# A state-space convolution mixed with a bilinear GLU: the last sums in another order, and the planner's durations as traced

## The chip, the cores and the metric

The kernel runs on one core of one Trainium2 chip. The metric is device time in microseconds (us) from the first to the last moment of one execution on the chip. Runs are repeated and the median is given. Beside the timed runs there is one profiled execution, whose trace records every instruction of every engine: TensorE (PE; its weight loads are listed apart as PEld), VectorE (DVE), ScalarE (ACT), GpSimd (POOL) and SyncE (SP). SP's queue issues most transfers, POOL's queue those that add to what lies in memory. A name that ends in q (SPq, POOLq) is an engine's sequencer, which issues transfers and waits.

## The reference

Two layers work on a sequence of 2048 tokens with 512 channels, and a gate mixes them:

```python
x = A_u                                              # [1, 2048, 512]
g = sigmoid((x * gate_w).sum(-1, keepdims=True))     # one number per token
# layer A: a state-space convolution (S4D), 128 modes per channel
dt = exp(log_dt);  A = -exp(log_A_real) + 1j * A_imag;  C = (C_real + 1j * C_imag) * dt
P = exp((A * dt)[:, :, None] * arange(2048))
K = 2 * einsum("dn,dnl->dl", C, P).real              # a kernel of 2048 taps per channel
a = irfft(rfft(x, 4096) * rfft(K, 4096))[:2048] + x * D_skip
# layer B: a GLU without nonlinearity, 1792 hidden units, on its own input
b = ((B_x @ w_gate) * (B_x @ w_up)) @ w_down
return g * a + (1 - g) * b
```

## The kernel before

**The GLU.** Three products in float32 quality: each operand is split into a rounded high part and a low remainder (`whi`, `wlo`, `xs`, `hh`, `hl`, `dhi`, `dlo`), and three matmuls of 128x128 by 512 replace one. The 14 tiles of the hidden dimension are worked in four groups (3, 3, 4, 4), and within a group the tokens in four chunks of 512, forwards in even groups and backwards in odd ones, so that the last chunk worked is chunk 0 (rows 0 to 3 of the output's `[128, 16, 512]` view, `LAST = 0`). For each chunk and tile there are the products `pg` and `pu`; ScalarE copies `pg` to `h`, VectorE multiplies by `pu`, and the result is split. The `y` products follow, and `evacuate` (line 563) scales them by 1 - g on ScalarE into `acc`. The first group stores `acc` to the output; later groups add to the output with an accumulating transfer from POOL's queue. Only for the last chunk of the last group does `acc` stay on the chip; its four rows are written by `ends` (line 581).

**The convolution.** Channels go in 16 blocks of 32. For each block VectorE and ScalarE build tables of powers (`phases`, `direct_powers`, `x_table`, `v_table`; tiles `t`, `rt`, `ri`, `su`, `di`, `x`, `v`, `sq`), and `k_block` (line 996) multiplies them into the taps `kt`. Four blocks make a channel block of 128 channels. For each of these (q = 0 to 3; "the third" is q = 2, "the fourth" q = 3) a transform in four steps follows: the input's and the taps' first step lies in memory as `su_d` and `sk_d`; `m_second` (line 1113) does the second step for each of four sets T; `m_product` multiplies in the frequency domain; `m_inverse` (line 1171) does the inverse's first step for two sets at once and stores it to `y_d`; `m_last` (line 1213) does the last step from `y_d`, for two halves g = 0 (rows 0 to 7) and g = 1 (rows 8 to 15).

`m_last` makes two banks of PSUM per half. ScalarE copies the odd bank, VectorE forms sum and difference with the even one, the rows are multiplied by the gate (`mix_act` on ScalarE for q < 3, `mix_dve` on VectorE for q = 3), and POOL adds them to the output with an accumulating transfer. For q = 2 and q = 3 half g = 0 is cut in two pieces: rows 0 to 3, which stay on the chip (`late["fin"]`), and rows 4 to 7, which are accumulated. In the trace, `m_last` for q = 2 is `k<-in,w_t` with results in tile `in`; for q = 3 it is `k<-x,w_t`, two groups of 16 matmuls with results in tile `x`. `m_inverse` is `k<-y,w3s`.

**The end.** `ends` loads rows 0 to 3 of the output, as far as they are summed, into `sums` (which takes the tile slot `kt`, 1 MB, by SP's queue), adds the two kept pieces for each row (q = 2 and q = 3, 128 columns each), then `acc`, and stores the row (256 KB, SP's queue).

**What sets the order.** Nothing is issued as the code is read. Every step is handed to a planner (`class Work`, line 165) with its engine, a duration in us, what it reads and writes, and a rank. `Work.run` (line 263) plays the steps through on paper: it takes the step that can start first, then the lower rank, then the earlier one in the code, keeps books of the tile slots, of PSUM banks (four of tag `k` for the convolution) and of one bus for transfers, and so makes one order for each engine. On the chip each engine follows its order, and the framework's semaphores make every step wait for its operands. So a duration in the code changes nothing in the instructions, only the order. `T_STEP` sets the earliest planned start of each GLU step, and `many=` keeps runs of many small matmuls apart. A tag's slots are handed out in the order in which the tiles were made in the code (line 240).

Of the kernel before, what the change touches and what calls it, by code (L numbers as in the profile page):

```python
# [18 lines left out]
P = 128  # L19
# [300 lines left out]
def gated_mix_kernel(  # L320
# [33 lines left out]
    m_su, m_sk, m_y, m_out, m_xs = (work.memory() for _ in range(5))  # L354
# [226 lines left out]
    def ends():  # L581
# [5 lines left out]
            w=[sums, *((m_out, t0 + r) for r in range(4))], dma=1024, rows=range(t0, t0 + 4),  # L587
        )
        for r, acc in ending:
            t = t0 + r  # L590
            for q, (fin, parts) in late["fin"].items():
                add(
                    "dve", 0.25,
                    lambda r=r, q=q, fin=fin: dve.tensor_tensor(
                        out=sums.t[:, r, P * q : P * q + P], in0=sums.t[:, r, P * q : P * q + P],
                        in1=fin.t[:, 4 * (LAST % 2) + r], op=ALU.add,
                    ),
                    r=parts, w=[(sums, (r, q))], rank=0,
                )
# [46 lines left out]
    def u_part(t):  # L646
# [4 lines left out]
        def score_of(j):  # L651
# [3 lines left out]
                "dve", 0.77,  # L655
# [191 lines left out]
    def phases(b):  # L847
# [3 lines left out]
        tt(0.83, lambda: t.t, lambda: per_power(rates()[:, 1]), lambda: per_channel(turns), ALU.mult, [par, m_powers], [t])  # L851
        add("act", 0.77, lambda: act.activation(rt.t, t.t, AF.Identity, bias=shift[:, 0:1]), r=[t, m_const], w=[rt])

        add(
            "dve", 0.83,
# [6 lines left out]
            "act", 2.13 if b % 2 or not b else 0.83, lambda: act.activation(t.t, t.t, AF.Sin, scale=-TWO_PI), w=[t],  # L862
        )
        add(
            "act", 0.83, lambda: act.activation(rt.t, rt.t, AF.Sin, scale=-TWO_PI, bias=half_pi[:, 0:1]), r=[m_const],
# [6 lines left out]
    def direct_powers(b):  # L872
# [4 lines left out]
        for c in range(2):  # L877
            f = t if c else rt
            tt(0.83, lambda c=c: ri.t[:, c], lambda f=f: f.t, ampl, ALU.mult, [f, e], [(ri, c)])
# [72 lines left out]
    def v_table(b):  # L952
# [8 lines left out]
        add("act", 1.28, copies, r=[ri], w=[(v, 2)])  # L961
# [5 lines left out]
        for to, of, n in (((33, 64, 2), (0, 16, 1), 16), ((34, 64, 4), (33, 49, 2), 8)):  # L967
# [11 lines left out]
            us = 0.04 * n + 0.08  # L979
            add("act", 1.15 if n == 16 else 0.73, sq_act, r=src_parts, w=[(v, ("r", k)), sq])  # L980
# [15 lines left out]
    def k_block(b, x, v):  # L996
# [18 lines left out]
        add("act", 0.4, lambda: act.copy(side(1), pv(0)[:, :, :, ::-1]), r=[pk], w=[(kt, (1, b % 4))])  # L1015
        for h, op in enumerate((ALU.add, ALU.subtract)):
            add(
                "dve", 0.4, lambda h=h, op=op: dve.tensor_tensor(out=side(h), in0=pv(1), in1=side(1), op=op),
# [52 lines left out]
    def evict(q, n, us, to, src, r, w):  # L1071

        if q == KT - 1 and n % 2:
            add("dve", us, lambda: dve.tensor_copy(to(), src()), r=r, w=w)
# [12 lines left out]
    def m_load(q, T):  # L1087
# [11 lines left out]
        for w, (src, m) in enumerate(((su_d, m_su), (sk_d, m_sk))):  # L1099
            for p in range(2):  # L1100
                r0 = 64 * p + 16 * T
                add(
                    "pool", 1.2,
# [310 lines left out]
```

## Time and profile before

| | |
|---|---|
| median of 3 runs | 606.57 us (606.55 to 610.38) |
| profiled execution | 608.69 us, its span from first to last instruction 606.9 us |
| TensorE busy | 586.3 us, 97% of the span |
| VectorE busy | 527.0 us, 87% |
| ScalarE busy | 389.8 us, 64% |
| POOL busy | 113.9 us, 19% |
| mean granted TensorE clock | 0.989 |
| transfers | 129.73 MB, 214 GB/s in the mean |

Each view of the profile has its own columns. In order of time: start, duration, engine, line, operation, tile written<-tiles read, shapes, count, and in brackets the idle time of the engine just before with what ended it. In groups: engine, operation, tiles, shapes, count, then busy us and mean ns of one, then idle time before them. In stretches: start:end and length, then for TensorE, weight loads, VectorE, ScalarE and POOL the busy us and in brackets the instructions, then the granted TensorE clock, the transfers' share and GB/s. The chain of waits is followed back from the last instruction and gives start, length and engine of each piece. For transfers: tiles, queue, count, KB of each, and us from issue to landing. Every instruction is recorded under line 119, that of a helper, so tiles tell them apart.

### The profile page before, as it was taken

The numbers are of one execution on the slowest core, as the hardware profiler recorded it, in microseconds if no ns is written. First come the engines' busy times: TensorE is split into PE (matmuls) and PEld (weight loads), VectorE is DVE, ScalarE is ACT, GpSimd is POOL, SyncE is SP. The second block draws the span as 40 slices with busy tenths as digits, with TensorE's granted clock in tenths as the row PEclk, the third lists the DMA queues.
The fourth block names the chain that finished last, engine by engine and source line by source line (L and its number), as shares of the span: only waits on it lengthen the run. The fifth ranks groups of instructions, "written<-read, shape, count | busy, mean of one in ns | idle before, by whom it ended". The sixth has DMA issues, their size and how long they took to land.

```text
span 606.9 us, 15872 instructions
## 1 busy us (share of the span) xinstructions
PE 586.3 (97%) x6500; PEld 444.8 (73%) x6500; DVE 527.0 (87%) x841; ACT 389.8 (64%) x879; POOL 113.9 (19%) x173
## 2 busy tenths in 40 slices
PE   8889999999999999999999999999899999999993
PEld 5657676787877777786687877866688777777772
DVE  6999999999999999999799999979999950775725
ACT  5279688686679588758958665966877423434621
POOL 0011212300201340201324101003424021402101
PEclk9989999999999999999999999999899999999997
DMA  8899978575647796749989827886989269989876
GB/s 278 313 354 341 360 263 326 161 218 162 136 151 206 211 226 192 161 135 283 237 178 228 185 81 192 198 228 178 204 171 234 63 170 343 207 257 232 214 155 121
DMA packets 69276, 129.73 MB, mean 214 GB/s; under 512 B 6868, under 2 KB 35540, under 8 KB 66772
## 3 DMA queue, kind: packets, MB, share of 16 engines
q1 hardware_dynamic: 47476, 88.21, 45.8%
q0 software_dynamic: 21312, 40.38, 33.1%
q8 instruction: 51, 0.84, 0.6%
q14 instruction: 21, 0.17, 0.1%
q10 hardware_dynamic: 416, 0.13, 0.1%
HBM read 73.65 MB, written 55.05 MB: 212 GB/s over the span
## 4 chain that ended last, share of the span: by engine, by line
PE 67%; DVE 16%; DMA 10%; issue 4%; ACT 2%; POOLq 0%; SPq 0%; ACTq 0%; DVEq 0%; POOL 0%
PE pg L119 19%; PE pu L119 18%; PE y L119 17%; PE k L119 13%; DMA raw<-in_wts 5%; DVE v L119 3%; DVE x L119 2%; DMA y_d<-e 2%; DMA dt_d<-small 2%; DVE wlo L119 1%; DVE y L119 1%; DVE ri L119 1%; DVE t L119 1%; DVE m L119 1%; DMA x<-dt_d 1%
## 5 line engine op out<-in xcount | busy, mean ns | idle before, releaser
L119 PE MATMUL pg<-xs,whi 128*128 128x512 f32 x448 | 140.1, 394 | 0.5 <-ACT whi L119 0.4
L119 PE MATMUL pu<-xs,whi 128*128 128x512 f32 x448 | 138.2, 390 | 0.0
L119 PEld LDWEIGHTS pg<-xs,whi 128*128 128x128 f32 x448 | 85.0, 190 | 19.8 <-ACT whi L119 1.9
L119 PEld LDWEIGHTS pu<-xs,whi 128*128 128x128 f32 x448 | 84.1, 188 | 17.0
L119 PE MATMUL pg<-xs,wlo 128*128 128x512 f32 x224 | 90.2, 403 | 4.3 <-ACT h L119 3.8
L119 PE MATMUL y<-dhi,hl 128*128 128x512 f32 x224 | 91.1, 407 | 2.9 <-ACT acc L119 1.8
L119 PE MATMUL y<-dlo,hh 128*128 128x512 f32 x224 | 88.2, 394 | 1.6 <-DVE dlo L119 1.6
L119 PE MATMUL pu<-xs,wlo 128*128 128x512 f32 x224 | 89.6, 400 | 0.0
L119 PE MATMUL y<-dhi,hh 128*128 128x512 f32 x224 | 87.9, 393 | 0.0
L119 POOL DMA_DIRECT2D out<-acc x44 | 38.7, 918 | 243.3 <-ACT acc L119 204.7
L119 ACT COPY ev<-k 128x512 f32<-128x512 f32 x112 | 59.2, 594 | 17.2 <-PE k L119 17.2
L119 ACT CAST hh<-h 128x512 fp32r<-128x512 f32 x56 | 34.8, 621 | 44.6 <-DVE h L119 44.4
L119 PEld LDWEIGHTS y<-dhi,hl 128*128 128x128 f32 x224 | 42.4, 189 | 24.3 <-issue 7.8
L119 ACT ACTIVATE acc<-y,ngate 128x512 f32<-128x512 f32 x63 | 42.7, 688 | 25.6 <-PE y L119 20.6
L119 PEld LDWEIGHTS pg<-xs,wlo 128*128 128x128 f32 x224 | 42.5, 190 | 21.5 <-ACT h L119 6.8
L119 PEld LDWEIGHTS pu<-xs,wlo 128*128 128x128 f32 x224 | 42.0, 188 | 15.7 <-issue 7.0
L119 ACT COPY h<-pg 128x512 f32<-128x512 f32 x56 | 32.9, 587 | 31.5 <-PE pg L119 26.1
L119 DVE TENSOR_TENSOR h<-pu,h 128x512 f32<-128x512 f32 x56 | 38.6, 689 | 16.6 <-PE pu L119 15.4
L119 PEld LDWEIGHTS y<-dlo,hh 128*128 128x128 f32 x224 | 42.4, 189 | 9.8 <-DVE dlo L119 1.9
L119 PEld LDWEIGHTS y<-dhi,hh 128*128 128x128 f32 x224 | 42.5, 190 | 9.2
L119 DVE TENSOR_TENSOR hl<-h,hh 128x512 fp32r<-128x512 f32 x56 | 38.5, 688 | 3.7 <-ACT hh L119 3.4
L119 POOL DMA_DIRECT2D su_d<-ev x32 | 17.4, 550 | 96.4 <-ACT ev L119 96.4
(124 smaller groups left out, 1004.2 us busy)
## 6 DMA issues: line engine op xcount, KB each, us to landing
xs<-xs_d SPq DMA_DIRECT2D x36, 512.0 KB, 6.0
out<-acc POOLq DMA_DIRECT2D x44, 256.0 KB, 6.4
raw<-in_wts SPq DMA_DIRECT2D x36, 256.0 KB, 3.7
xs_d<-xs SPq DMA_DIRECT2D x16, 512.0 KB, 7.9
su_d<-ev POOLq DMA_DIRECT2D x32, 256.0 KB, 6.1
y_d<-ts SPq DMA_DIRECT2D x14, 512.0 KB, 4.9
in<-su_d POOLq DMA_DIRECT2D x24, 256.0 KB, 7.9
sk_d<-ev SPq DMA_DIRECT2D x6, 1024.0 KB, 5.6
```

Source lines behind the costliest of these rows:

```text
L119: got = getattr(self.engine, name)(*args, **kw)
```

## The change

- A marker `m_turn` is written by each `m_inverse` and read by `m_last` of q = 2, which so comes after the second `m_inverse` of q = 3.
- In `m_last` the piece that is accumulated (rows 4 to 7) comes ahead of the kept one (rows 0 to 3). The kept pieces are no longer multiplied by the gate; `ends` does that together with the sum, in one `scalar_tensor_tensor` per row and channel block.
- For q = 3 the loads from `y_d` for half g = 1 stand ahead of those for g = 0.
- The load of `sums` comes after the first `y_d` store of q = 3.
- Some fifteen durations that the planner is given are changed.

```diff
--- before.py
+++ after.py
@@ -351,7 +351,7 @@
     sk_d = dram.tile([KT, P, 32, P], F32, name="sk_d")
     y_d = dram.tile([KT, P, 32, P], F32, name="y_d")
     xs_d = dram.tile([4, KT, P, 2, D], F32, name="xs_d")
-    m_su, m_sk, m_y, m_out, m_xs = (work.memory() for _ in range(5))
+    m_su, m_sk, m_y, m_out, m_xs, m_turn = (work.memory() for _ in range(6))
 
     pools = {n: open_pool(n, b, PSUM) for n, b in (("ps_y", 2), ("ps_g", 1), ("ps_k", 4))}
     const = open_pool("const")
@@ -584,18 +584,18 @@
         sums = new("tab", "kt", [P, 4, D])
         add(
             "sp", 0.42, lambda: sp.dma_start(sums.t, ov[:, t0 : t0 + 4, :]),
-            w=[sums, *((m_out, t0 + r) for r in range(4))], dma=1024, rows=range(t0, t0 + 4),
+            r=[(m_y, (KT - 1, 0))], w=[sums, *((m_out, t0 + r) for r in range(4))], dma=1024, rows=range(t0, t0 + 4),
         )
         for r, acc in ending:
             t = t0 + r
             for q, (fin, parts) in late["fin"].items():
                 add(
                     "dve", 0.25,
-                    lambda r=r, q=q, fin=fin: dve.tensor_tensor(
-                        out=sums.t[:, r, P * q : P * q + P], in0=sums.t[:, r, P * q : P * q + P],
-                        in1=fin.t[:, 4 * (LAST % 2) + r], op=ALU.add,
+                    lambda r=r, q=q, t=t, fin=fin: dve.scalar_tensor_tensor(
+                        sums.t[:, r, P * q : P * q + P], fin.t[:, 4 * (LAST % 2) + r], gate[:, t : t + 1],
+                        sums.t[:, r, P * q : P * q + P], op0=ALU.mult, op1=ALU.add,
                     ),
-                    r=parts, w=[(sums, (r, q))], rank=0,
+                    r=[*parts, (m_gate, LAST)], w=[(sums, (r, q))], rank=0,
                 )
             add(
                 "dve", 0.69,
@@ -652,7 +652,7 @@
             r = 4 * t + j
             pr = new("mid", "y", [P, D], bufs=2)
             add(
-                "dve", 0.77,
+                "dve", 0.73,
                 lambda: dve.scalar_tensor_tensor(
                     pr.t, ut.t[:, j, :], 1.0, gw.t, op0=ALU.mult, op1=ALU.mult, accum_out=gate[:, r : r + 1]
                 ),
@@ -848,21 +848,21 @@
 
         t, rt = (new("tab", n, FULL) for n in ("t", "rt"))
         par, rates = pars[b][0]
-        tt(0.83, lambda: t.t, lambda: per_power(rates()[:, 1]), lambda: per_channel(turns), ALU.mult, [par, m_powers], [t])
-        add("act", 0.77, lambda: act.activation(rt.t, t.t, AF.Identity, bias=shift[:, 0:1]), r=[t, m_const], w=[rt])
+        tt(0.85, lambda: t.t, lambda: per_power(rates()[:, 1]), lambda: per_channel(turns), ALU.mult, [par, m_powers], [t])
+        add("act", 0.86, lambda: act.activation(rt.t, t.t, AF.Identity, bias=shift[:, 0:1]), r=[t, m_const], w=[rt])
 
         add(
-            "dve", 0.83,
+            "dve", 0.85,
             lambda: dve.scalar_tensor_tensor(t.t, rt.t, ROUND, t.t, op0=ALU.subtract, op1=ALU.subtract),
             r=[rt], w=[t],
         )
 
         add("act", 0.77, lambda: act.activation(rt.t, t.t, AF.Abs), r=[t], w=[rt])
         add(
-            "act", 2.13 if b % 2 or not b else 0.83, lambda: act.activation(t.t, t.t, AF.Sin, scale=-TWO_PI), w=[t],
+            "act", 2.07 if b % 2 or not b else 0.77, lambda: act.activation(t.t, t.t, AF.Sin, scale=-TWO_PI), w=[t],
         )
         add(
-            "act", 0.83, lambda: act.activation(rt.t, rt.t, AF.Sin, scale=-TWO_PI, bias=half_pi[:, 0:1]), r=[m_const],
+            "act", 0.85, lambda: act.activation(rt.t, rt.t, AF.Sin, scale=-TWO_PI, bias=half_pi[:, 0:1]), r=[m_const],
             w=[rt],
         )
         polar[b] = t, rt
@@ -876,7 +876,7 @@
         ri = ris[b] = new("tab", "ri", [P, 2, TB, NP])
         for c in range(2):
             f = t if c else rt
-            tt(0.83, lambda c=c: ri.t[:, c], lambda f=f: f.t, ampl, ALU.mult, [f, e], [(ri, c)])
+            tt(0.85, lambda c=c: ri.t[:, c], lambda f=f: f.t, ampl, ALU.mult, [f, e], [(ri, c)])
 
         su, di = sus[b] = new("tab", "su", [P, TB, 18]), new("tab", "di", [P, TB, 11])
         re, im = (lambda a, c=c: ri.t[:, c, :, a:18] for c in range(2))
@@ -958,7 +958,7 @@
                 act.copy(v.t[:, c, :, 0:4], ri.t[:, c, :, W_B])
                 act.copy(v.t[:, c, :, 36::4], ri.t[:, c, :, W_A])
 
-        add("act", 1.28, copies, r=[ri], w=[(v, 2)])
+        add("act", 1.46, copies, r=[ri], w=[(v, 2)])
         outer(
             v, lambda: ri.t[:, :, :, W_A], lambda: su.t[:, :, W_A], lambda: ri.t[:, :, :, W_B],
             lambda: su.t[:, :, W_B], lambda: di.t[:, :, 0:4], [ri, su, di],
@@ -976,8 +976,8 @@
 
             k = 0 if n == 16 else 1
             src_parts = [(v, ("r", 0)), (v, ("i", 0))] if k else [(v, 0), (v, 1), (v, 2)]
-            us = 0.04 * n + 0.08
-            add("act", 1.15 if n == 16 else 0.73, sq_act, r=src_parts, w=[(v, ("r", k)), sq])
+            us = 0.69 if n == 16 else 0.63
+            add("act", 1.17 if n == 16 else 0.89, sq_act, r=src_parts, w=[(v, ("r", k)), sq])
             add(
                 "dve", us,
                 lambda dst=dst, src=src: dve.scalar_tensor_tensor(
@@ -1012,10 +1012,10 @@
         add("pe", 2.15, kgen, r=[x, v], w=[pk], rank=0, hold=[kt], many=work.APART)
         pv = lambda a: pk.t.rearrange("p (g a b k) -> p g a b k", a=2, b=2, k=16)[:, :, a]
         side = lambda h: kt.t[:, h, :, g0 : g0 + 8].rearrange("p b g k -> p g b k")
-        add("act", 0.4, lambda: act.copy(side(1), pv(0)[:, :, :, ::-1]), r=[pk], w=[(kt, (1, b % 4))])
+        add("act", 0.37, lambda: act.copy(side(1), pv(0)[:, :, :, ::-1]), r=[pk], w=[(kt, (1, b % 4))])
         for h, op in enumerate((ALU.add, ALU.subtract)):
             add(
-                "dve", 0.4, lambda h=h, op=op: dve.tensor_tensor(out=side(h), in0=pv(1), in1=side(1), op=op),
+                "dve", 0.42, lambda h=h, op=op: dve.tensor_tensor(out=side(h), in0=pv(1), in1=side(1), op=op),
                 r=[pk, (kt, (1, b % 4))], w=[(kt, (h, b % 4))], rank=0,
             )
         if b % 4 == 3:
@@ -1071,7 +1071,7 @@
     def evict(q, n, us, to, src, r, w):
 
         if q == KT - 1 and n % 2:
-            add("dve", us, lambda: dve.tensor_copy(to(), src()), r=r, w=w)
+            add("dve", us + 0.1, lambda: dve.tensor_copy(to(), src()), r=r, w=w)
         else:
             add("act", us, lambda: act.copy(to(), src()), r=r, w=w)
 
@@ -1100,7 +1100,7 @@
             for p in range(2):
                 r0 = 64 * p + 16 * T
                 add(
-                    "pool", 1.2,
+                    "pool", 0.88,
                     lambda w=w, src=src, p=p, r0=r0: pool_q.dma_start(
                         at()[64 * p : 64 * p + 64, :, w], src[q, r0 : r0 + 16].rearrange("(j e) n d -> (e n) j d", e=2)
                     ),
@@ -1190,7 +1190,7 @@
                                     ys[t].t[lanes, k, e, cs], start=k == 0, stop=k == 1, tile_position=(32 * j, 64 * e),
                                 )
 
-        add("pe", 2.13, fn, r=[*ys, *ws], w=banks, rank=1, hold=sts, many=apart_of(q))
+        add("pe", 2.13, fn, r=[*ys, *ws], w=[*banks, (m_turn, (q, T0))], rank=1, hold=sts, many=apart_of(q))
         for j in range(4):
             st, m = sts[j // 2], j % 2
             evict(
@@ -1228,7 +1228,7 @@
                         r=[(m_y, (q, T)) for T in range(4)], w=[(t, p)], dma=512,
                     )
             src.append(t)
-            cuts = ((0, 1), (1, 1)) if q >= KT - 2 and g == LAST // 2 else ((0, 2),)
+            cuts = ((1 - LAST % 2, 1), (LAST % 2, 1)) if q >= KT - 2 and g == LAST // 2 else ((0, 2),)
             to = t if q >= KT - 2 else stage([P, 8, P])
             pieces += [(g, to, *cut) for cut in cuts]
 
@@ -1244,7 +1244,7 @@
                         )
 
         add(
-            "pe", 0.2 + 0.86 * len(gs), fn, r=[*src, m_w4], w=[b for bs in banks for b in bs], rank=1,
+            "pe", 0.2 + 0.86 * len(gs), fn, r=[*src, m_w4, *([(m_turn, (KT - 1, 2))] if q == KT - 2 else [])], w=[b for bs in banks for b in bs], rank=1,
             hold=[to for _, to, _, _ in pieces],
         )
         cs = slice(P * q, P * q + P)
@@ -1279,11 +1279,11 @@
                     op=ALU.mult,
                 )
 
-            args = ("dve", 0.15 + 0.54 * n, mix_dve) if q == KT - 1 else ("act", 1.14 * n, mix_act)
-            add(*args, r=[(m_gate, r // 4) for r in range(r0, r0 + 4 * n, 4)], w=parts)
             if n == 1 and n0 == LAST % 2:
                 late.setdefault("fin", {})[q] = t, parts
                 continue
+            args = ("dve", 0.15 + 0.54 * n, mix_dve) if q == KT - 1 else ("act", 1.22 * n, mix_act)
+            add(*args, r=[(m_gate, r // 4) for r in range(r0, r0 + 4 * n, 4)], w=parts)
             rs = list(range(r0, r0 + 4 * n))
             add(
                 "pool", 0.95,
@@ -1315,7 +1315,7 @@
                 done = []
         if q == KT - 1:
             late["y"] = [new("tab", "x", [P, 16, P], bufs=2) for _ in range(2)]
-            for g in range(2):
+            for g in (1 - LAST // 2, LAST // 2):
                 for half in range(2):
                     for p in range(2):
                         lanes = slice(64 * p + 32 * half, 64 * p + 32 * half + 32)
```

## The prediction

> **What bounds the kernel now.** I read the page's busy shares first, then the busy time in stretches of 20 us, then the last microseconds in order of time.
>
> ```profile
> PE 586.3 (97%) x6500; PEld 444.8 (73%) x6500; DVE 527.0 (87%) x841; ACT 389.8 (64%) x879; POOL 113.9 (19%) x173
> ...
> 20.00:40.00 20.00, 15.75 (x71) 11.52 (x71) 19.33 (x36) 9.48 (x33) 0.00 (x0) 0.91 0.87 310
> ...
> 100.00:120.00 20.00, 18.43 (x92) 14.01 (x92) 18.83 (x27) 14.31 (x25) 4.92 (x9) 1.00 0.63 231
> ...
> 420.00:440.00 20.00, 17.67 (x147) 11.58 (x145) 19.23 (x28) 14.73 (x35) 10.02 (x12) 0.91 1.07 198
> ...
> 560.00:580.00 20.00, 20.00 (x230) 15.15 (x230) 12.66 (x23) 11.40 (x29) 2.84 (x2) 1.00 0.96 228
> 580.00:600.00 20.00, 17.45 (x99) 12.26 (x97) 10.43 (x20) 5.29 (x10) 1.98 (x2) 1.00 0.58 124
> ```
>
> After the stretch, the first pair is TensorE; the column before the last two is its granted clock. TensorE is idle 4.25 us in 20 to 40, 1.57 in 100 to 120, 2.33 in 420 to 440 (with a clock of 0.91), and hardly elsewhere until about 597. The end is set by TensorE's sum of work plus what follows its last matmul:
>
> ```profile
> 597.07 0.39 PE L119 MATMUL y<-dhi,hh 128*128 128x512 f32 x1
> 597.49 0.69 ACT L119 ACTIVATE raw<-y,ngate 128x512 f32<-128x512 f32 x1 [2.03 <-PE y L119]
> 597.66 1.23 DVE L119 TENSOR_TENSOR x<-x,gate 128x1024 f32<-128x1024 f32 x1
> 598.80 0.68 DVE L119 TENSOR_TENSOR kt<-raw,kt 128x512 f32<-128x512 f32 x1
> 599.31 1.54 POOL L119 DMA_DIRECT2D out<-x  x1 [3.91 <-DMA out<-kt]
> ...
> out<-x POOLq DMA_DIRECT2D x1, 512.0 KB, 6.5
> out<-kt SPq DMA_DIRECT2D x1, 256.0 KB, 2.0
> ```
>
> The last two rows are the transfers issued from 598 on, with microseconds to landing. TensorE ends at 597.07 + 0.39 = 597.46; the span is 606.9, so the tail is 9.44 us. In it VectorE first multiplies eight rows by the gate, which delays the last row's sum, and the accumulating 512 KB transfer of those rows lands last: 599.31 + 6.5 = 605.8, and 1.1 us closes the program. The last row's own store landed at 598.80 + 0.68 + 2.0 = 601.5. So some 4 us of tail belong to rows 8 to 15 of the fourth block, not to the GLU's last row.
>
> **The change, part by part.** First the order of the fourth block's last sets. In the chain of waits and in time:
>
> ```profile
> 561.31 1.95 PE L119 MATMUL k<-in,w_t 64*32 64x512 f32 x32
> 563.95 1.28 DVE L119 TENSOR_TENSOR y<-y,ev 128x512 f32<-128x512 f32 x2
> 570.22 2.10 PE L119 MATMUL k<-y,w3s 32*64 32x128 f32 x128
> ...
> 573.70 10.25 DMA y_d<-e
> 584.33 4.06 DMA x<-y_d
> ...
> 589.46 1.09 PE L119 MATMUL k<-x,w_t 64*32 64x512 f32 x16
> 591.06 1.42 DVE L119 TENSOR_TENSOR x<-k,x 128x256 f32<-128x256 f32 x4 [4.79 <-ACT x L119]
> 591.37 1.09 PE L119 MATMUL k<-x,w_t 64*32 64x512 f32 x16
> ...
> 596.22 1.41 DVE L119 TENSOR_TENSOR x<-k,x 128x512 f32<-128x512 f32 x2
> ```
>
> The third block's last set (561.31) holds four PSUM banks ahead of the fourth's second inverse (570.22), whose inputs are ready at 565.23. Put behind it (the m_turn edge, from line 1193 to line 1246), the inverse may go up to 5 us earlier; the same 32 matmuls are only moved. Their accumulating transfers go with them:
>
> ```profile
> 570.41 1.28 POOL L119 DMA_DIRECT2D out<-in  x1 [12.18 <-ACT in L119]
> ...
> out<-in POOLq DMA_DIRECT2D x1, 512.0 KB, 10.8
> y_d<-ri SPq DMA_DIRECT2D x1, 512.0 KB, 5.6
> y_d<-e SPq DMA_DIRECT2D x1, 512.0 KB, 10.2
> ```
>
> Today POOL's 512 KB is in flight while SP's y_d<-e takes 10.2 us, against 5.6 for its twin. Behind the inverse they come later; the store then costs 5.6 to 10.2, and I take 5.6, its twin's row: 4.6 us earlier. Together the last sets can start 0 to 9.6 us earlier. None of this shortens the run by itself, because TensorE has GLU matmuls beside it without a gap; it decides only whether the rest is hidden. Of the two sets, rows 8 to 15 (g = 1) are now loaded and meant to go first, so their sums (the pair of 1.41 at 596.22) start when the other set's do today, at 591.06; with the mix they end at 591.06 + 1.41 + 1.23 = 593.7, POOL follows 0.4 later as at 599.31, and the 512 KB land at 594.1 + 6.5 = 600.6, even without the earlier start.
>
> The tail is then the GLU's last row alone: 597.49 + 0.69 on ScalarE, 0.03 for the hand-over (as 597.46 to 597.49), 0.68 on VectorE = 598.9, SP's issue, landing, 1.1 of close. For the landing the four stores of this kind give the bounds:
>
> ```profile
> DMA to landing us min/median/max: 2.0/3.7/3.9
> ```
>
> That is 598.9 + 2.0 + 1.1 = 602.0 to 598.9 + 3.9 + 1.1 = 603.9: the tail shortens by 4.9 to 3.0 us. I take **3.9**, the middle, as 2.0 was measured once and 3.7 is the median. [...]
>
> Gate and sum in one operation:
>
> ```profile
> L119 DVE TENSOR_TENSOR kt<-kt,x 128x128 f32<-128x128 f32 x4 | 1.0, 281 | 0.0
> L119 DVE SCALAR_TENSOR_TENSOR v<-v 128x512 f32<-128x512 f32 x16 | 11.0, 689 | 0.0
> L119 DVE SCALAR_TENSOR_TENSOR v<-v 128x256 f32<-128x256 f32 x16 | 10.1, 630 | 0.0
> L119 ACT ACTIVATE in<-in,gate 128x128 f32<-128x128 f32 x16 | 5.0, 390 | 1.0 <-DVE in L119 0.8
> L119 DVE TENSOR_TENSOR x<-x,gate 128x512 f32<-128x512 f32 x2 | 1.3, 682 | 0.0
> ```
>
> Eight sums of 128x128 become scalar_tensor_tensor. At 128x512 that form costs what tensor_tensor does (0.69 against the 0.68 at 598.80), so I take 281 ns each; the far bound is the strided 630, or 8 x 0.35 = 2.8 us on VectorE. Gone are four gate copies on ScalarE (1.56 us) and one mix on VectorE (0.68). VectorE is busy 12.66 and 10.43 of the last two 20 us and all but the last row's sums precede 597: cost and gain are both nothing on the path, and up to 2.8 us if that cover is gone.
>
> The load of the sums moves behind the fourth block's first y_d store on SP:
>
> ```profile
> 501.40 0.33 SPq L119 DMA_DIRECT2D kt<-out  x1
> 516.10 2.13 POOL L119 DMA_DIRECT2D x<-sk_d  x3 [4.18 <-DMA sk_d<-e]
> 554.85 6.59 SPq L119 DMA_DIRECT2D y_d<-ts  x2
> ...
> kt<-out SPq DMA_DIRECT2D x1, 1024.0 KB, 8.9
> ```
>
> One megabyte leaves the way of sk_d<-e, for which POOL waited 4.18 us; that is slack, as TensorE was full. Issued at about 561.4 it lands near 570.3; the fourth block's pieces reach the sums only after 589.46, so 19 us cover it. Behind it on SP stand the x<-y_d loads; it waits for nothing still running, so it costs them its 0.33 us of issue and up to 8.9 of shared bandwidth, hidden by the GLU matmuls.
>
> Last, the durations. They enter the planner only, not the instructions, but shift its order everywhere. Per channel block, the planner's VectorE gets 0.46 more for two 128x256 operations (0.40 to 0.63, as the 630 above), 0.12 for six small edits of 0.02, and 0.06 less for two of 128x512: 0.5 us, or 8 over 16 blocks. Real VectorE time is unchanged, so Fourier and table work goes later among GLU matmuls in TensorE's order. Its cost lies in stalls, and the trace has one to price:
>
> ```profile
> 432.68 0.50 PE L119 MATMUL pg<-xs,wlo 128*128 128x512 f32 x1 [2.02 <-ACT h L119]
> ...
> 432.68 4.59 PE pg L119 x12
> 452.03 2.72 PE pu L119 x12
> ...
> 434.00:436.00 2.00, 2.00 (x6) 1.54 (x6) 1.73 (x3) 2.00 (x7) 1.15 (x2) 0.50 1.38 164
> ```
>
> TensorE stood 2.02 us; the next twelve matmuls, at a granted clock of 0.50, took 4.59 where twelve take 2.72, so such a stall costs 2.02 + 1.87 = 3.9 us. The bounds for the new order are one stall fewer and two more, -3.9 to +7.8; I take zero, as TensorE's waits in the middle are few and nothing says which way they go. [...]
>
> **Sum.** Tail -3.9, fused operations 0, load 0, order 0: -3.9. The profiled execution took 608.69 (span 606.9, 1.8 around it), so it would take 604.8. The median of the runs is 606.57, 2.1 below it; from that, **602.7**.
>
> **Rivals.** *One stall more in the middle.* For: VectorE is busy 19 of 20 us there, so a late operand has no spare time to be made in. Against: truer durations should avoid it. 602.7 + 3.9 = 606.6; two, 610.5.
>
> *The stall at 430 goes.* For: it came from a late copy on ScalarE, in an order planned with too fast a VectorE. Against: any order has its own. 602.7 - 3.9 = 598.8.
>
> *The fourth block overhangs the GLU.* Slower. Today 597.46 - 592.46 = 5.0 us of GLU stand behind the last set (591.37 + 1.09). If the order lets the sets slip the 8 us of the durations and the up to 9.6 us do not come, TensorE ends 3 us late on them. Then follow, from rows above, both pieces' sums and one mix on VectorE (1.42 + 0.68 = 2.1), four fused (1.1), four row sums (2.7), a store and the close (3.9 + 1.1): 10.9 against 9.44. 606.57 + 3.0 + 1.5 = 611.1. It decides from 5 us of slip. Against: TensorE takes GLU matmuls only where nothing else can start.
>
> *It does not do what it says.* Both destinations share the tag "x" in turn, and g = 0 was made first, so g = 1's loads can't be first of all. If its set still goes last, the 512 KB are again the last thing to land: 606.6.
>
> **How the numbers follow.** Forecast (600.5 to 605.5) 0.42; one stall more 0.20 and two 0.06; stall gone 0.13; overhang 0.11; not done 0.08. One per cent is 6.07 us, about what a measurement of this kernel can tell from no change: 600.5 and 612.6. Faster by over that: most of the stall gone and the forecast's lower edge, 0.15. Slower: half the overhang and part of two stalls, 0.09. Within: 0.76. The range 598.3 to 611.5 leaves out about half of the stall gone, half the overhang and some of two stalls, under 2 in 10. The forecast's own range stands within 1% and below the time before.
>
> **What would show it.** Right: in the end's order of time, the 512 KB out<-x well before the last matmul; a row store as the last transfer; a tail of 4.6 to 6.5 us; the inverse ahead of k<-in; y_d<-e near 5.6 us; kt<-out behind y_d<-ts. TensorE's last matmul within 1 us of 597.5 would show the middle untouched. Wrong: a dip of the granted clock at a new place, an x<-gate mix behind the last y matmul, or fused sums far over 281 ns.

## The result and the profile after

The changed kernel takes **611.98 us** in the median of 9 runs (608.98 to 613.63), the kernel before 606.83 beside it: a ratio of 1.0076, with a 95% interval of 1.0052 to 1.0099. It is slower by 0.8%, where 602.7 was forecast, and lies just above the range. The profiled execution took 611.92 us, with a span of 610.1 against 606.9.

The first view is TensorE's busy time in stretches of 20 us, for the changed kernel (start:end, length, TensorE's busy us and matmuls, granted clock, transfers' share, GB/s), and then the same for the kernel before where the forecast did not show it:

```profile
120.00:140.00 20.00, 18.11 (x196) 1.00 0.64 175
...
420.00:440.00 20.00, 19.54 (x259) 1.00 1.11 208
...
520.00:540.00 20.00, 18.96 (x254) 1.00 1.04 265
...
560.00:580.00 20.00, 18.41 (x345) 1.00 1.04 272
...
sum 600.00, PE 586.29; mean PE 19.54
```

```profile
120.00:140.00 20.00, 20.00 (x208) 1.00 0.69 182
...
520.00:540.00 20.00, 20.00 (x265) 1.00 0.94 224
```

TensorE's busy time is the 586.3 us of before. The stall at 430 is gone (19.54 busy at full clock, 17.67 at 0.91 before), but gaps of 1.0 to 1.9 us stand at three other places, 120, 520 and 560, that were full. The end of the changed kernel in order of time:

```profile
591.13 1.09 PE L119 MATMUL k<-x,w_t 64*32 64x512 f32 x16
...
592.95 1.42 DVE L119 TENSOR_TENSOR x<-k,x 128x512 f32<-128x512 f32 x2 [2.63 <-DMA x<-y_d]
...
595.79 1.09 PE L119 MATMUL k<-x,w_t 64*32 64x512 f32 x16
...
597.39 1.42 DVE L119 TENSOR_TENSOR x<-k,x 128x256 f32<-128x256 f32 x4 [1.77 <-DMA out<-in]
598.41 2.85 POOL L119 DMA_DIRECT2D out<-x  x2 [5.17 <-DVE x L119]
...
598.76 0.40 PE L119 MATMUL y<-dhi,hh 128*128 128x512 f32 x1
599.20 0.69 ACT L119 ACTIVATE raw<-y,ngate 128x512 f32<-128x512 f32 x1 [1.56 <-PE y L119]
599.33 0.60 DVE L119 SCALAR_TENSOR_TENSOR kt<-x,gate,kt 128x128 f32<-128x128 f32 x2
599.85 1.28 DVE L119 TENSOR_TENSOR kt<-acc,kt 128x512 f32<-128x512 f32 x2
600.56 4.57 SPq L119 DMA_DIRECT2D out<-kt  x4
...
602.18 0.68 DVE L119 TENSOR_TENSOR kt<-raw,kt 128x512 f32<-128x512 f32 x1
```

TensorE's last matmul ends at 598.76 + 0.40 = 599.16, 1.7 us later than the 597.46 of before, and the tail behind it is 610.1 - 599.16 = 10.94 us instead of 9.44. These 1.7 and 1.5 are the whole 3.2 us between the two spans. The half g = 1 is first now, as meant; but its set ends at 592.22 and the other one only at 596.88, with 2.3 us of GLU behind it, where before had 5.0. All of VectorE's work for four rows then follows, to 602.18 + 0.68 = 602.86, which is 3.70 us behind the last matmul, and another 7.24 us pass from there to the end. What was in flight in these 7.24 us is told by the transfers issued from 595 on (tiles, queue, count, KB of each, us to landing):

```profile
out<-kt SPq DMA_DIRECT2D x4, 256.0 KB, 5.1
out<-x POOLq DMA_DIRECT2D x1, 512.0 KB, 6.3
out<-x POOLq DMA_DIRECT2D x1, 256.0 KB, 7.9
```

The four row stores and both accumulating transfers, 1.8 MB together, start within 598.41 to 605.13.

### The profile page after: what moved, and what is told of

The parts are those of the page before. It is cut to its first block, busy times and chain, and to the rows that moved or that the text cites. A ratio compares the mean times of both kernels' runs of the same rounds, so it can differ in the third digit from the quotient of the medians.

```text
span 610.1 us, 15873 instructions
## 1 busy us (share of the span) xinstructions
PE 586.3 (96%) x6500; PEld 444.2 (73%) x6500; DVE 527.0 (86%) x840; ACT 389.6 (64%) x875; POOL 113.9 (19%) x173
## 4 chain that ended last, share of the span: by engine, by line
PE 65%; issue 15%; DMA 10%; DVE 5%; ACT 2%; POOL 2%; SPq 0%; DVEq 0%; POOLq 0%; ACTq 0%
PE pg L119 19%; PE y L119 17%; PE pu L119 17%; PE k L119 12%; DMA w2s<-in_w 2%; DMA in<-sk_d 2%; DMA in<-y_d 2%; DMA dt_d<-small 1%; POOL out L119 1%; DMA y_d<-ts 1%; DMA out<-in 1%; DVE y L119 1%; DVE v L119 1%; DMA x<-dt_d 1%; POOL in L119 1%
## 5 line engine op out<-in xcount | busy, mean ns | idle before, releaser
L119 POOL DMA_DIRECT2D out<-acc x44 | 40.2, 961 | 243.2 <-ACT acc L119 238.3
L119 PEld LDWEIGHTS k<-v,x 128*32 128x32 f32 x2048 | 30.6, 109 | 6.6 <-issue 5.1
```

Of the source, the lines that this page charges most:

```text
L119: got = getattr(self.engine, name)(*args, **kw)
```

## Experiments

Two theories at first. **S, the slip:** the new durations make the planner put the convolution later among the GLU matmuls, the last sets slip, and what VectorE does behind them lies behind the GLU. **R, the moved transfers:** the order is harmless, and the load of the sums and the accumulating transfers cost the time at their new places.

### The two halves of the change

The change without its new durations (**order_only**, an excerpt; the other durations go back in the same way):

```diff
-        tt(0.85, lambda: t.t, ...
+        tt(0.83, lambda: t.t, ...
...
-            us = 0.69 if n == 16 else 0.63
-            add("act", 1.17 if n == 16 else 0.89, sq_act, ...
+            us = 0.04 * n + 0.08
+            add("act", 1.15 if n == 16 else 0.73, sq_act, ...
...
-                    "pool", 0.88,
+                    "pool", 1.2,
```

> The changed kernel with every duration of the planner as before: only the new order of the last sums is left. In its TensorE order 18 GLU matmuls (4.1 us) stand behind both last sets of the fourth block; before it was 24 and 21, in the changed kernel 24 and 9. Theory S (the durations let tables and transforms slip later among the GLU matmuls, the last set comes too near the end, and VectorE's sums with four row stores are laid bare): 605.5 to 608.5, near the time before, as the slip is gone but 4.1 us still don't cover VectorE's 9 us behind the sets. Theory R (the moved transfers and the new order of the sums cost the time, the durations do nothing): 610 to 613.

Measured: 609.53 us (607.38 to 612.7) beside 607.75 for the kernel before, 1.0031 [1.0013, 1.0049]. That lies between the two forecasts, 1.0 us above S's and 0.5 below R's. Its end in order of time:

```profile
591.22 1.95 PE L119 MATMUL k<-x,w_t 64*32 64x512 f32 x32
...
593.03 1.75 DVE L119 TENSOR_TENSOR x<-k,x 128x512 f32<-128x512 f32 x3 [6.77 <-ACT x L119]
...
596.41 2.85 POOL L119 DMA_DIRECT2D out<-x  x2 [14.10 <-DVE x L119]
...
597.10 0.39 PE L119 MATMUL y<-dhi,hh 128*128 128x512 f32 x1
...
598.66 4.52 SPq L119 DMA_DIRECT2D out<-kt  x4
...
600.27 0.69 DVE L119 TENSOR_TENSOR kt<-raw,kt 128x512 f32<-128x512 f32 x1
```

TensorE ends at 597.49, as before (597.46). But the tail is 608.2 - 597.49 = 10.71 us, nearly the changed kernel's 10.94. So the reordered end is longer than the old one without the new durations too. Its sets do stand a little later: both start at 591.22, where those of before started at 589.46 and 591.37, and they have 4.3 us of GLU behind them, not 5.0. VectorE works without a gap from 593.03 to 600.96; that is 3.47 us behind the last matmul, and 7.24 us follow, as in the changed kernel. By the medians, some 2 us of the loss are here. The rest comes with the durations; in the traces it is TensorE's later end (1.7 us), and hardly the tail.

The other half, the kernel before with the new durations alone (**durations_only**, an excerpt):

```diff
-        tt(0.83, lambda: t.t, ...
+        tt(0.85, lambda: t.t, ...
...
-            us = 0.04 * n + 0.08
+            us = 0.69 if n == 16 else 0.63
```

> The kernel before with the changed durations alone; the last sums in the old order. No GLU matmul is left behind the last sets, and the last table product stands behind 1704 of 2016 GLU matmuls as in the changed kernel, not 1653. Theory S: slower than the changed kernel, 612 to 617. Theory R: 606 to 608.

Measured: 618.26 us (614.0 to 621.54), 1.0171 [1.0138, 1.0203], above even S's 612 to 617. TensorE's last matmuls are now these, in order of time:

```profile
599.12 3.28 PE L119 MATMUL k<-x,w_t 64*32 64x512 f32 x32
```

Both last sets stand behind the whole GLU, the first 599.12 - 589.46 = 9.7 us later than before, and the tail is 617.1 - 602.40 = 14.7 us. Only the order on the engines can have done this, as no instruction differs. That refutes R's first half: the durations are not harmless. The durations of the two squarings are enough (**order_squares**):

```diff
 # the change without its new durations, but
-            us = 0.04 * n + 0.08
-            add("act", 1.15 if n == 16 else 0.73, sq_act, ...
+            us = 0.69 if n == 16 else 0.63
+            add("act", 1.17 if n == 16 else 0.89, sq_act, ...
```

> The new order of the last sums with one of the changed durations, that of the two squarings per channel block (0.40 to 0.63 on VectorE). In the planner's order it lets the last table product slip behind 1722 GLU matmuls instead of 1653, and no GLU matmul is left behind the last sets. Theory S (slip lays the tail bare): 613 to 618, slower than the changed kernel. Rival (it takes all durations together, or other stalls of theirs): 607 to 611.

Measured: 622.1 us (619.41 to 622.76) beside 607.95, 1.0225 [1.0195, 1.0256]; the direction as expected, the size larger. Again no GLU stands behind the last set, and the tail is 14.9 us. This part of the new durations costs more alone than all of them together: the planner's order doesn't follow the sum of the edits.

### What the edge gains

The changed kernel without the m_turn edge, so that the third block's last set may go ahead of the fourth's second inverse again (**after_no_turn**):

```diff
-        add("pe", 2.13, fn, r=[*ys, *ws], w=[*banks, (m_turn, (q, T0))], rank=1, ...
+        add("pe", 2.13, fn, r=[*ys, *ws], w=banks, rank=1, ...
...
-            r=[*src, m_w4, *([(m_turn, (KT - 1, 2))] if q == KT - 2 else [])], ...
+            r=[*src, m_w4], ...
```

> The changed kernel without the edge that puts the third block's last set behind the fourth's second inverse; all else as changed, and only the last part of TensorE's order differs. No GLU matmul is left behind the last sets (24 and 9 in the changed kernel). Theory S: 614 to 619, so the edge itself gains. Rival (the third block's late accumulations are what costs): 606 to 610.

Measured: 617.34 us (616.78 to 618.98), 1.016 [1.0132, 1.0187], as expected. Against 1.0076 with the edge, it is worth about 0.8%, 5 us. Without it no GLU stands behind the last sets: the last four x<-y_d loads are issued at 593.35 where the changed kernel's are at 586.75, the sets start at 596.76, and the tail is 14.6. The changed kernel's rows show what the edge does:

```profile
578.63 2.09 PE L119 MATMUL k<-y,w3s 32*64 32x128 f32 x128
...
582.11 0.39 SPq L119 DMA_DIRECT2D y_d<-e  x1
582.91 1.95 PE L119 MATMUL k<-in,w_t 64*32 64x512 f32 x32
```

```profile
y_d<-e SPq DMA_DIRECT2D x1, 512.0 KB, 4.6
```

The inverse is ahead of the third block's set, y_d<-e takes 4.6 us instead of 10.2, and from the inverse's end (580.72) to the first last set (591.13) it is 10.4 us instead of 17.1. But the inverse itself starts at 578.63, 8.4 us later than the 570.22 of before. The last table product shows the slip ahead of it, first before and then after:

```profile
486.72 2.07 PE L119 MATMUL k<-v,x 128*32 128x64 f32 x128
```

```profile
496.58 2.07 PE L119 MATMUL k<-v,x 128*32 128x64 f32 x128
```

It is 9.9 us later. So the edge's gain was there, and the durations used it up.

### Cover behind the last sets

If S holds, the predicted tail should come as soon as enough GLU work stands behind the last sets. `T_STEP` plans the GLU later, so that the convolution ends earlier among it. First in the change without its new durations (**order_paced**), then in the changed kernel itself (**after_paced**):

```diff
-T_STEP = 9.85
+T_STEP = 10.1
```

> As order_only, with the pace of the GLU steps in the planner at 10.1 us in place of 9.85, so that 51 and 48 GLU matmuls (11.6 and 10.9 us) stand behind the two last sets. Theory S: VectorE's 9 us behind the sets are covered, the tail behind the last matmul is 4.6 to 6.5 us as predicted, and the time 602 to 605 unless the middle stalls. Theory R: 610 to 613, as all moved transfers are in it.

```diff
-T_STEP = 9.85
+T_STEP = 10.25
```

> The changed kernel, durations and all, with the pace of the GLU steps in the planner at 10.25 us: 39 and 36 GLU matmuls (8.8 and 8.2 us) behind the two last sets, not 24 and 9. Theory S: a tail of 5 to 7.5 us and 604 to 608, though the durations are in it. Theory R: 610 to 613.

Measured: 606.73 us (604.39 to 608.57), 0.9978 [0.9959, 0.9996], with a tail of 4.82 us; and 607.87 us (605.53 to 610.48), 1.0005 [0.9987, 1.0024], with a tail of 5.13. Both have the tail that was predicted, 4.6 to 6.5, and the changed kernel's is halved. The load of the sums and the accumulating transfers behind the inverse are at their new places in both, so these alone, as R had it, don't make the tail. What they gain there, they give back in the middle, so that the first misses S's 602 to 605. Its SP loads and TensorE's longest wait, in order of time:

```profile
536.03 2.38 SPq L119 DMA_DIRECT2D in<-y_d  x4
...
538.51 0.52 SPq L119 DMA_DIRECT2D w2s<-in_w  x1
...
548.57 2.46 PE L119 MATMUL k<-v,w2s 32*32 32x256 f32 x64 [3.93 <-DMA w2s<-in_w]
```

The load of a 128 KB matrix, w2s, which depends on nothing computed, stood on SP's queue behind loads that waited for a store to land (y_d<-ts, 14.42 us in the chain of waits). Issued at 538.51, beside 3.5 MB of other loads, it landed only 9.9 us later. TensorE stood 3.93 us for it, and the granted clock was 0.83 in that stretch of 20 us. With the fourth block's w2s loads on ScalarE's queue, in the same TensorE order (**order_paced_actw**):

```diff
-    def w_load(tag, shape, src):
+    def w_load(tag, shape, src, q=0):
...
-        add("sp", 0.42, lambda: sp.dma_start(t.t, src), w=[t], dma=256, after=150.0)
+        e, queue = ("act", act) if q == KT - 1 else ("sp", sp)
+        add(e, 0.42, lambda: queue.dma_start(t.t, src), w=[t], dma=256, after=150.0)
...
-                w_load("w2s", ...),
+                w_load("w2s", ..., q),
```

> The re-paced new order with the fourth block's w2s weights issued from ScalarE's queue, so that they no longer stand behind the loads of y_d on SP. TensorE's order is the same; in the re-paced run it stood 3.9 us for w2s, and its granted clock fell. If that wait is a cost of its own beside the tail, it goes with its slow clock: 4 to 6 us less than the 606.7 of the re-paced order, 601 to 603. If TensorE only waits somewhere else: 605 to 608.

Measured: **602.52 us** (600.97 to 603.92, 6 runs) beside 607.95, 0.991 [0.9887, 0.9933]: faster than both kernels. That it lies at the forecast's 602.7 is chance, as pace, queue and durations are other ones and TensorE ends 1.8 us earlier (595.71) than before. With w2s on ScalarE's queue, the matmuls that follow it start at 544.30, not 548.57, without a wait, and the granted clock from 540 to 560 is 1.00. Its end:

```profile
583.12 1.09 PE L119 MATMUL k<-x,w_t 64*32 64x512 f32 x16
...
595.32 0.39 PE L119 MATMUL y<-dhi,hh 128*128 128x512 f32 x1
...
596.47 0.69 DVE L119 TENSOR_TENSOR kt<-raw,kt 128x512 f32<-128x512 f32 x1 [2.02 <-ACT raw L119]
```

11.5 us of GLU stand behind the last set. The last sum ends 1.45 us behind the last matmul, and the end comes 3.34 us later.

Is it the pace and the queue alone? The same two edits on the kernel before (**before_paced_actw**), and the queue's alone on that one (**before_actw**) and on the changed kernel (**after_actw**):

> The kernel before with the pace of 10.1 us in place of 9.85 and the fourth block's w2s on ScalarE's queue: what the 602.5 us kernel has beside the reordering and the old durations. Its last sets have 24 and 21 GLU matmuls (5.4 and 4.8 us) behind them, as before, and not 51 and 48. Theory V (the tail is VectorE's list behind the last set, with the stores beside the accumulating transfers; it shortens only where some 8 us of GLU stand behind that set): tail 9.3 to 9.8 us, and the time that of the kernel before within 0.4%, so that the reordering is what gains 4 to 5 us once it has the cover. If pace and queue alone make the gain: tail near 5 us and 602 to 603.

Measured: 606.99 us (606.28 to 609.6), 0.9977 [0.9957, 0.9997], with a tail of 9.56. Without the reordering the pace leaves the sets where they were.

> The kernel before with the fourth block's w2s loads issued from ScalarE's queue; TensorE's order of work is the same as before. Before, TensorE waited for no w2s there. Theory S: within 0.3% of the kernel before (605.5 to 608.5 where that takes 607), tail near 9.4 us, so that the 602.5 of the paced order needs the order and the pace, and the queue only takes away the stall that they made. If the queue alone is worth 4 us: near 603.

Measured: 607.59 us (605.92 to 609.03), 0.9973 [0.9956, 0.999], tail 9.67. The queue's edit is worth up to 0.3% by itself, so of the 0.9% some 0.6%, 4 us, belong to the reordering with its cover.

> The changed kernel, with the fourth block's w2s loads issued from ScalarE's queue in place of SP's; TensorE's order of work is the same, last set with 9 GLU matmuls (2.0 us) behind it. In the changed kernel TensorE stood 1.04 us at 538 for w2s and 1.58 us with no releaser at 571. Theory S (the slip makes the tail): the tail stays at 10.5 to 11.2 us, and only the middle can gain: 1 to 2.6 us less than the 611.98 of the changed kernel, 609.4 to 611, so that it is still not faster than before. If the queue alone makes the gain seen with the paced order (4 us there), this kernel gains 4 as well: near 608 and a ratio near 1.000.

Measured: 610.89 us (609.31 to 612.63), 1.0039 [1.0022, 1.0056], tail 10.7. One to two us of the changed kernel's loss go with the queue's edit: in the trace its wait of 1.04 us for w2s is gone, but the one that has no releaser, 1.58 us near 570, stays (1.7 us), so this one isn't the queue's. The tail doesn't depend on either.

### What the tail is made of

Two causes are bunched in the changed kernel's tail: VectorE's list, and transfers that meet. The changed kernel without the fourth block's two accumulating transfers takes only the second away (**after_no_accum**):

```diff
             rs = list(range(r0, r0 + 4 * n))
+            if q == KT - 1:
+                continue
             add(
                 "pool", 0.95,
```

> The changed kernel without the two accumulating transfers of the fourth block; rows 4 to 15 of its 128 channels lack the convolution. Every engine's order is the same but for these two. In the changed kernel the four row stores took 4.8 to 5.7 us beside them. If sharing with the 768 KB is a part of the tail, the stores land in 2 to 4 us and the time is 2 to 3.5 us shorter, 608 to 610; if VectorE's sums alone set the tail, 611 to 612.5.

Measured: 606.81 us (605.54 to 611.49), 0.9997 [0.9974, 1.002]; 1.2 us less than the low end of what was expected. Its end in order of time, and its row stores from issue to landing:

```profile
597.15 0.40 PE L119 MATMUL y<-dhi,hh 128*128 128x512 f32 x1
...
600.57 0.69 DVE L119 TENSOR_TENSOR kt<-raw,kt 128x512 f32<-128x512 f32 x1
```

```profile
out<-kt SPq DMA_DIRECT2D x4, 256.0 KB, 2.0
```

The last sum still ends 3.71 us behind the last matmul (601.26 - 597.55), but only 3.44 us follow in place of 7.24. So 3.8 us of the tail is what the row stores lose beside the accumulating transfers. The two spans, 604.7 and 610.1 us, differ by 1.6 us more, as TensorE ends at 597.55 and not at 599.16; the edit doesn't explain that.

By then the theory was **V**: the tail is VectorE's list behind the last set, 7.8 us from its end, and the stores beside the accumulating transfers; it shortens only where some 8 us of GLU cover both. (In the changed kernel, whose first set runs 4.7 us ahead of the second, the list is 602.86 - 596.88 = 6.0 us.) A point between the covers tried so far is the 602.5 us kernel without the edge (**order_paced_actw_no_turn**):

> The 602.5 us kernel without the edge that puts the third block's last set behind the fourth's second inverse. Its last sets have 30 and 27 GLU matmuls (6.8 and 6.1 us) behind them, between the 18 that left a tail of 10.7 us and the 36 that left 5.1. Theory V: VectorE's list of 7.8 us from the end of the last set ends 1.5 to 2.0 us behind the last matmul, little over the floor of 1.45, and the stores still meet part of the accumulating transfers, 5 to 7.2 us to the end: tail 6.5 to 9 us, and 604 to 607. If the tail went by the edge itself and not by the cover: 10.5 to 11, near 608.5.

```profile
592.73 1.09 PE L119 MATMUL k<-x,w_t 64*32 64x512 f32 x16
...
599.78 0.39 PE L119 MATMUL y<-dhi,hh 128*128 128x512 f32 x1
...
600.92 0.69 DVE L119 TENSOR_TENSOR kt<-raw,kt 128x512 f32<-128x512 f32 x1 [0.83 <-ACT raw L119]
```

Measured: 608.51 us (607.08 to 611.39), 1.0004 [0.9987, 1.0021]. The tail is 607.7 - 600.17 = 7.53 us, within V's 6.5 to 9, and its first part is down at 1.44; the time missed the expected 604 to 607, because TensorE waited in the middle for other loads (17.20 of 20 us busy at 540) and ended late. The ends together, in us, worked out from the rows of each (durations_only is left out, as its last sum isn't VectorE's last operation):

| kernel | GLU behind the last set | last sum behind last matmul | from there to the end | tail |
|---|---|---|---|---|
| order_squares | 0 | 7.79 | 7.15 | 14.9 |
| after_no_turn | 0 | 7.10 | 7.49 | 14.6 |
| changed | 2.3 | 3.70 | 7.24 | 10.9 |
| after_actw | 2.3 | 3.69 | 7.01 | 10.7 |
| after_no_accum | 2.3 | 3.71 | 3.44 | 7.2 |
| order_only | 4.3 | 3.47 | 7.24 | 10.7 |
| order_paced_actw_no_turn | 6.4 | 1.44 | 6.09 | 7.5 |
| after_paced | 8.8 | 1.44 | 3.69 | 5.1 |
| order_paced | 11.5 | 1.45 | 3.37 | 4.8 |
| order_paced_actw | 11.5 | 1.45 | 3.34 | 4.8 |
| before, old order of the halves | 5.0 | 2.02 | 7.42 | 9.4 |
| before_actw, old order | 5.0 | 2.03 | 7.64 | 9.7 |
| before_paced_actw, old order | 5.0 | 2.03 | 7.53 | 9.6 |

In the new order both parts shrink as the cover grows. The first is down at 1.44 from 6.4 us of cover on; the second falls from 6.1 to 3.7 between 6.4 and 8.8.

## Why the prediction was wrong

**The step that failed is the tail's sum, "the tail is then the GLU's last row alone".** It rested on "VectorE is busy 12.66 and 10.43 of the last two 20 us and all but the last row's sums precede 597". The first is an average over 20 us. VectorE in the kernel before, in the last 8 of them:

```profile
591.06 1.42 DVE L119 TENSOR_TENSOR x<-k,x 128x256 f32<-128x256 f32 x4 [4.79 <-ACT x L119]
592.40 1.28 DVE L119 TENSOR_TENSOR x<-x,gate 128x512 f32<-128x512 f32 x2
593.60 0.48 DVE L119 TENSOR_TENSOR kt<-kt,x 128x128 f32<-128x128 f32 x2
594.00 1.28 DVE L119 TENSOR_TENSOR kt<-acc,kt 128x512 f32<-128x512 f32 x2
595.21 0.48 DVE L119 TENSOR_TENSOR kt<-kt,x 128x128 f32<-128x128 f32 x2
595.62 0.68 DVE L119 TENSOR_TENSOR kt<-acc,kt 128x512 f32<-128x512 f32 x1
596.22 1.41 DVE L119 TENSOR_TENSOR x<-k,x 128x512 f32<-128x512 f32 x2
597.66 1.23 DVE L119 TENSOR_TENSOR x<-x,gate 128x1024 f32<-128x1024 f32 x1
598.80 0.68 DVE L119 TENSOR_TENSOR kt<-raw,kt 128x512 f32<-128x512 f32 x1
```

From 591.06 to 599.48 no gap is over 0.03 us. VectorE was the bound of the end already. The second half of the sentence was true only because half g = 0 came first: three of the four rows' sums went ahead of the other half's two operations. With these two first, the end of the list is all four rows' sums, with the four stores behind them. In the traces the last sum then ends 3.5 to 3.7 us behind the last matmul, not the 1.44 of the forecast, and 7.24 us follow, not the 3.1 to 5.0 of "SP's issue, landing, 1.1 of close". Together this is 10.7 to 10.9 us for the 4.6 to 6.5 forecast. Of the 5.4 us by which the changed kernel's tail misses the sum's 5.5 (9.44 - 3.9), 2.3 are VectorE's list and 3.1 the stores.

**The landing of the stores was the larger part.** The bounds of 2.0 to 3.9 came from stores of which three had one accumulating transfer of 256 KB beside them, and the fourth, the 2.0, was issued only 0.2 us behind the one of 512 KB. With both accumulating transfers and all four stores in the same 7 us the median was 5.1 (5.4 in order_only); without the accumulating ones 2.0.

How much would remain with the sets where they were? As an estimate, the forecast's start of VectorE's list, 591.06, and order_only's length of it, 7.9 us, end at 599.0, close to the 598.9 of the forecast. Behind it come the 6.1 and 7.2 us measured with 6.4 and 4.3 us of cover. That is a tail of 7.6 to 8.7 us, less than before's 9.44 but far from the forecast's. No run has the new order with these places of the sets.

**The 512 KB were late for another reason too.** The forecast had them issued at 594.1 and landed at 600.6; they were issued at 598.41 and landed 6.3 us later. Their rows were ready at 594.40 + 1.22 = 595.62, 1.9 us later than forecast, as the set ran later. In order_only POOL followed 0.5 us behind that point. Here the third block's transfer to the same rows, which the edge had put behind the late inverse, was still in flight:

```profile
591.68 1.55 POOL L119 DMA_DIRECT2D out<-in  x1 [1.73 <-ACT in L119]
...
out<-in POOLq DMA_DIRECT2D x1, 512.0 KB, 6.4
```

It landed at 598.08, 0.33 us ahead of 598.41. The profile names VectorE as what POOL waited for, but the rows had long been done, so the transfer is the likely cause. This much of R is left. What it costs is not measured; order_only has the same 7.24 us without it.

**The overhang rival had the mechanism, and the wrong point.** "It decides from 5 us of slip" counted TensorE's cover alone. In order_only the first set is 1.8 us later than before and the last one's end 0.7, and the tail is already longer than before. The tail of 4.8 to 5.1 us appeared only with 8.8 us of GLU and more behind the last set, and the kernel before had 5.0. Its price of 10.9 us for the tail came out at 10.94, but by luck: it had 5.9 us of VectorE behind TensorE's end and 5.0 for store and close, and measured were 3.70 and 7.24. TensorE didn't end late on the sets (the GLU still ended last), and in place of the 3 us it gave to that there were 1.7 us of waits in the middle.

**Order at zero was half right.** The slip by the durations was taken as 8 us, and was 9.7 us in durations_only and 9.9 us at the changed kernel's last table product. The gain set against it, "0 to 9.6 us earlier", came: 10.4 us from inverse to set instead of 17.1, y_d<-e at 4.6 us. Together they left the first set 1.7 us later than before and the second 4.4. In the middle the stall at 430 went (the second rival), three others came (the first), and TensorE ended 1.7 us later, inside the -3.9 to +7.8 that was given.

**Fused operations:** 281 ns were taken, and the rows say more (count, then min/median/max ns):

```profile
L119 DVE SCALAR_TENSOR_TENSOR kt<-in,gate,kt x4: 339/342/347, 589.2 to 590.0; 128x128 f32<-128x128 f32 x4
L119 DVE SCALAR_TENSOR_TENSOR kt<-x,gate,kt x4: 343/344/344, 599.3 to 601.3; 128x128 f32<-128x128 f32 x4
```

Four of them stand in the uncovered list: 4 x 62 = 0.25 us, which "nothing on the path" left out. The load of the sums is where it was said to be, and no engine is seen waiting for it; its issue on SP took 5.71 us instead of 0.33, and it landed after 12.4 us, not 8.9.

**The signs.** Of those named as right, the inverse ahead of k<-in, y_d<-e (4.6 us), the place of kt<-out and a row store as the last transfer are there; the early 512 KB, the tail and TensorE's end within 1 us of 597.5 are not.

**The time around.** Against the profiled execution the forecast was 604.8, and it was 611.92: 7.1 us, which are 5.4 of tail and 1.7 of the middle. The other 2 us of the miss come from taking the 2.1 us between before's profiled execution and its median over to the changed kernel, whose profiled execution lies at its median. What stays open is the share of each new gap in the middle: only the queue of w2s was tried, and the order they come from changes with any duration.

## What to carry to other kernels

Before work is moved to the end of an engine's list, write that list out from the last producer on, row by row, for each engine; a busy share over 20 us hid 8 us without a gap. In these runs the tail was down at 4.8 to 5.1 us only with 8.8 us and more of GLU behind the last set, and 9.4 us and more in every kernel that had 5.0 us or less and both accumulating transfers. So measure what follows the last producer, its operations and its transfers, against the work that another engine still has, and make that cover, as the pace did here. Where durations only feed a planner, better ones are a change of order like any other: take the position of the last producer in the new order, not the sign of the correction.

## What the runs showed of the hardware

- The 256 KB row stores from SP's queue landed in 2.0 us in the median without the fourth block's accumulating transfers (after_no_accum), and beside their 768 KB from POOL's queue in 5.1 us (the changed kernel), 5.4 (order_only, after_no_turn) and 5.5 (order_paced_actw_no_turn). Their issue took longer too, 332 to 363 ns in after_no_accum and in the changed kernel:

```profile
L119 SPq DMA_DIRECT2D out<-kt x4: 362/1215/1432, 600.6 to 603.7; - x4
```

  (ns, min/median/max).
- In order_paced a 128 KB load that needs nothing stood on SP's queue behind loads that waited for a store, landed 9.9 us after its issue beside 3.5 MB of others, and TensorE stood 3.93 us for it. With it on ScalarE's queue (order_paced_actw) TensorE did not wait for it, and its matmuls started at 544.30 and not at 548.57.
- TensorE's wait of 1.58 us at 569 to 571 in the changed kernel stands beside a granted clock of 1.00 in its stretch, that of 2.02 us in the kernel before beside 0.91 from 420 to 440 (0.50 from 434 to 436), and 3.93 us in order_paced beside 0.83 from 540 to 560. But the changed kernel also has a wait of 1.99 us that ends at 27.88, with 1.00 in every 2 us from 26 to 34, and the kernel before one of 1.85 us that ends at 33.55, with 0.50 from 34 to 36. So the length of the wait alone doesn't decide it here.
- scalar_tensor_tensor with a scalar per partition took 342 to 344 ns at 128x128, where tensor_tensor took 281 by the row in the forecast; at 128x512 the two had been alike (0.69 and 0.68 us).
